# An adaLN block with Hedgehog attention and a ReLU feed-forward: moving the feature work of two blocks ahead wholly into FFN1, and its attention products to the second and eighth part of FFN2

## The chip, the cores and the metric

The kernel runs on one core of a Trainium2 chip. The metric is the device time of one execution in microseconds (us), taken as the median over runs. Beside it stands one profiled execution, from which all durations of single instructions come.

## The reference, cut to what matters

```python
# S = 2048 rows, D = 576, H = 32 heads of 18, Dff = 4608, bf16 inputs
mod = (silu(c) @ w_mod).reshape(1, 6, 1, 576);  sa, ca, ga, sb, cb, gb = its six rows
h = layernorm(x) * (1 + ca) + sa
q, k, v = split(h @ wqkv)                                  # per head
phi(t) = concat(softmax(t @ w_phi), softmax(-(t @ w_phi)))  # 36 features a head
kv = phi(k)^T v;  z = sum over rows of phi(k)
o = (phi(q) kv) / (phi(q) z + 1e-6)
x = x + ga * (o @ wo)
h = layernorm(x) * (1 + cb) + sb
out = x + gb * (relu(h @ w1) @ w2)
```

## The kernel before

The 2048 rows are 16 tiles of 128. A first part (some 130 us) folds the modulation into the weights, projects all queries, keys and values, and builds `kv`. After it the rows go through in eight **blocks** of two tiles (`n` = 0 to 7, 256 rows each). Block 0 is part of a hand-written list of steps; blocks 1 to 7 are calls of `block(n)`. The program writes the order of TensorE (PE), VectorE (DVE), ScalarE (ACT) and of the DMA queue on SyncE (SP) by hand: each engine takes its instructions strictly as the code issues them, and waits only on semaphores.

A block has two stages on PE. **FFN1** (`ffn1_rows`) makes nine tiles `ps_h` of hidden units, each in an a-half and a b-half of the weight rows; they are issued as a0, a1, b0, a2, b1, ... a8, b7, b8. After each b-half ACT empties the tile with a ReLU (`f1_relu`, L872) into `H1`. The pool behind `ps_h`, `ps_y` has three buffers. A dictionary `behind` names what is issued right behind a given half: `("b", 5)` means behind the b-half of tile 5 and its ReLU. **FFN2** is twelve **parts** of twelve matmuls (`ffn2_step(n, j, cs, cn, part)`, L910): for each of the two row tiles `j` and each half of the columns `cs`, three parts; behind the third, DVE multiplies by the gate and adds the residual (L918, L919).

Between these matmuls three blocks are worked on at once. While block `n` is on PE:

- for block `m = n + 1`: the attention output projection (`wo_rows`, in two halves of rows, tile `ps_wo`), the residual `wo_out` and the row statistics `stats` (together `late`), and then `norm_out`: `rstd` on ACT (a logarithm and an exponential, L233, L234), `norm` and a copy on DVE (L238, L423) and two DMA transposes on SP into `hT` (L425). `mods` (L418 on DVE) then applies shift and scale to `hT`, which FFN1 of the next block reads.
- for block `n + 2`: the **features** of its queries in a buffer that the profile calls `room`: `low` and `high` (DVE), `exps(0)` and `exps(1)` (ACT, L506), `sums(0)` and `sums(1)` (DVE, L524, into `ln_s`), `recip` (ACT, L529 and L531, into `rsum`), `scale` (DVE, L541), `q_T` (two DMA transposes on SP into `ET`, one for each row tile, L653). Then `attention(n + 2, j)`: the products `num` on PE (L666: eleven small matmuls that read `ET`, into `ps_num` and `ps_nun`), `quotient` on DVE (L674 to L681) and a DMA transpose `o_T` on SP (L689).

Blocks 1 to 5 have all of this; block 6 has no features to make (`n + 2` is past the end), block 7 neither. In block 1 the attention of block 2 also falls into FFN1.

Of the kernel before, what the change touches and what calls it, by code (L numbers as in the profile page):

```python
# [21 lines left out]
NQ = NT // U  # L22
# [21 lines left out]
def kernel(  # L44
# [34 lines left out]
    def mm_tile(name):  # L79
        return mmp.tile([P, 2, 512], FP32, name=name, tag="mm")  # L80

    def aux_tile(name, dt=FP32):
        t = aux.tile([P, 512], FP32, name=name, tag="aux")
        return t if dt == FP32 else t.bitcast(BF16)
# [365 lines left out]
    HALVES = [(0, 288), (288, 288)]  # L450
# [148 lines left out]
    def q_soft(n):  # L599
        E = Eqs[n % 2]  # L600
        if n < 2:
            G.memset(E[:, :, :, DW:], 0.0)
        Es[n] = E
        b, u = n // 2, n % 2
        return softmax_parts(E[:, :, :, 0:DW], pq[b][:, u * U:(u + 1) * U], U, False)
# [42 lines left out]
    def q_T(n):  # L648
        E = Es[n]
        ET = work.tile([P, NG, U, P], BF16, name="ET", tag="ET", bufs=2)  # L650
        ETs[n] = ET
        for j in range(U):
            nc.sync.dma_start_transpose(out=ET[:, :, j, :], in_=E[:, j].rearrange("p g c -> p (g c)"))  # L653

    def num(n, j):

        ET = ETs[n]
        if n == 0:
            ps = mm_tile("ps_num")
            ps = (ps[:, 0], ps[:, 1])  # L660
        else:
            ps = (aux_tile("ps_num"), aux_tile("ps_nun"))
        onum[n, j] = ps
        for g in range(NG):
            o = (g % GB) * GV
            T_.matmul(ps[g // GB][:, o:o + gcols(g)], lhsT=ET[0:DW, g, j, :], rhs=KVZ[0:DW, g, 0:gcols(g)],  # L666
                      start=True, stop=True)
# [156 lines left out]
    def row_halves(key, phase, items):  # L824

        for k, (ps, l, r) in enumerate(items):
            i = T_.matmul(ps, lhsT=l, rhs=r, start=(phase == 0 and k < 2), stop=(phase == 1 and k >= len(items) - 2))  # L827
            if phase == 1 and k == 0:
                tc.add_manual_dep(i.ins, last[key].ins.name, AFTER, reason="same banks, other rows")
        if phase == 0:  # L830
            g = last[key] = G.memset(token[:], 0.0)  # L831
            tc.add_manual_dep(g.ins, i.ins.name, AFTER, reason="products of one half of the rows done")

    def f1_rows(n, q, phase):

        hT, w, items = hT2[n], U * P, []
        if phase == 0:
            f1_open(n, (q,))
        for hh in range(2):
            for ci in ((4, 0, 1, 2, 3) if phase == 0 else (0, 1, 2, 3)):  # L840
                for r in range(2):
                    s, e = slice(r * 64, r * 64 + 64), r ^ phase
                    l = w1["c"][s, 2 * q + hh, :] if ci == 4 else w1_at(2 * q + hh, e, ci, s)
                    items.append((f1[q][:, e, hh * w:hh * w + w], l, hT[s, ci, :]))
        row_halves(("f1", q), phase, items)

    def wo_rows(n, j, phase):

        if phase == 0:
            onum["wo", n, j] = [aux_tile("ps_wo") for _ in HALVES]  # L850
        items = []
        for ci in ((4, 0, 1, 2, 3) if phase == 0 else (0, 1, 2, 3)):
            for r in range(2):
                s, e = slice(r * 64, r * 64 + 64), r ^ phase
                items.append((onum["wo", n, j][e][:, 0:288], oTs[n, j][s, ci, :], wo_sb[s, ci, e * 288:e * 288 + 288]))
        row_halves(("wo", j), phase, items)

    def ffn1_rows(n, behind={}):

        for k in range(NI // 2 + 1):  # L860
            for p in (0, 1):
                q = k - p
                if k == 0 and p == 1 or q > NI // 2 - 1:
                    continue
                f1_rows(n, q, p)
                if p:
                    f1_relu(q)
                if ("ab"[p], q) in behind:
                    behind["ab"[p], q]()

    def f1_relu(q):
        A_.activation(out=p2t["H1"].rearrange("p (e j) n -> p e j n", e=2)[:, :, 2 * q:2 * q + 2],  # L872
                      in_=f1[q][:].rearrange("p e (h n) -> p e h n", h=2), func=ACT.Relu)
# [27 lines left out]
    def ffn2_step(n, j, cs, cn, part):  # L901

        if part == 0:
            f2[j, cs] = mm_tile("ps_y")
            if ("o", n, j) not in f2:
                f2["o", n, j], f2["sent"] = p2t["p2"].tile([P, D], BF16, name="outt", tag="outt", bufs=2), 0
        ps, o = f2[j, cs], f2["o", n, j]
        c = slice(cs, cs + cn)
        for k in [e * NI + part * 6 + i for e in range(2) for i in range(6)]:
            T_.matmul(ps[:, 0, 0:cn], lhsT=p2t["H1"][:, k, j * P:(j + 1) * P], rhs=p2t["w2"][:, k, c],  # L910
                      start=(k == 0), stop=(k == NJ - 1))
        if part == 2 and n > 0:
            ffn2_out(n, j, cs, cn)

    def ffn2_out(n, j, cs, cn):
        ps, o = f2[j, cs], f2["o", n, j]
        c = slice(cs, cs + cn)
        V.tensor_tensor(out=o[:, c], in0=ps[:, 0, 0:cn], in1=rows["gb"][:, c], op=ALU.mult)  # L918
        V.tensor_tensor(out=o[:, c], in0=o[:, c], in1=x_sb[:, n * U + j, c], op=ALU.add)  # L919
        if cs + cn == D or (n, j) == (NQ - 1, U - 1):  # L920
            nc.sync.dma_start(outv[:, n * U + j, f2["sent"]:cs + cn], o[:, f2["sent"]:cs + cn])
            f2["sent"] = cs + cn if cs + cn < D else 0

    def y(n, j, cols=HALVES):
        for cs, cn in cols:
            for part in range(3):
                ffn2_step(n, j, cs, cn, part)
# [74 lines left out]
    def block(n):  # L1002


        m = n + 1 if n + 1 < NQ else None
        if m is None:
            ffn1_rows(n)
            y(n, 0)

            y(n, 1, ((0, 288), (288, 192), (480, 96)))  # L1010
            return
        soft_ = q_soft(n + 2) if n + 2 < NQ else None
        xn, stats, rstd, norm = norm_stats(m * U, U)

        def do(name, *a):
            if soft_ is not None:
                getattr(soft_, name)(*a)

        def attention(m, j):
            num(m, j)  # L1020
            quotient(m, j)
            o_T(m, j)

        def late(j):
            wo_rows(m, j, 1)
            wo_out(m, j)
            stats(j)

        def norm_out():
            rstd()  # L1030
            norm()
            norm_dma(xn, U, new_hT2(m), 0)

        def mods():
            for ci in range(KC):
                modulate(V, hT2[m][:, ci, :], hT2[m][:, ci, :], mod[2], ci)

        def both(*fs):
            return lambda: [f() for f in fs]

        if n == 1:
            do("low")
            do("high")
            ffn1_rows(n, {("b", 0): lambda: attention(m, 0), ("b", 2): lambda: attention(m, 1), ("b", 3): lambda: do("exps", 0),
                          ("b", 4): both(lambda: wo_rows(m, 0, 0), lambda: do("exps", 1)), ("b", 5): both(lambda: late(0), lambda: do("sums", 0)),
                          ("a", 8): lambda: wo_rows(m, 1, 0), ("b", 7): lambda: late(1)})
        else:
            ffn1_rows(n, {("a", 0): both(lambda: do("low"), lambda: do("high")), ("b", 1): lambda: wo_rows(m, 0, 0),
                          ("b", 2): lambda: late(0), ("b", 3): lambda: do("exps", 0), ("b", 4): both(lambda: wo_rows(m, 1, 0), lambda: do("exps", 1)),
                          ("b", 5): both(lambda: late(1), lambda: do("sums", 0))})  # L1050
        norm_out()
        do("sums", 1)
        y(n, 0, HALVES[:1])
        do("recip", 0)
        do("scale", 0)
        if n + 2 < NQ:
            q_T(n + 2)
        ffn2_step(n, 0, 288, 288, 0)
        mods()
        ffn2_step(n, 0, 288, 288, 1)  # L1060
        ffn2_step(n, 0, 288, 288, 2)
        ffn2_step(n, 1, 0, 288, 0)
        if n + 2 < NQ:
            attention(n + 2, 0)
        ffn2_step(n, 1, 0, 288, 1)
        ffn2_step(n, 1, 0, 288, 2)
        ffn2_step(n, 1, 288, 288, 0)
        if n + 2 < NQ:
            attention(n + 2, 1)
        ffn2_step(n, 1, 288, 288, 1)  # L1070
        ffn2_step(n, 1, 288, 288, 2)

    for n in range(1, NQ):
        block(n)
# [28 lines left out]
```

## Time and profile before

| | |
|---|---|
| time, median of 3 runs | 415.11 us (414.38 to 416.61) |
| profiled execution: its own time | 414.88 us |
| profiled execution: its span | 413.1 us (1.8 us lie around it) |
| DVE, ACT busy share of the span | 57%, 43% |
| FFN1 of blocks 1 to 7 begins at | 140.6, 181.9, 220.8, 259.4, 298.1, 336.7, 374.4 us |

Times within the profile are microseconds from the start of the span. A timeline row has start, duration, engine, line, instruction, tiles (output <- inputs), shape and the number of instructions merged; what stands in brackets at its end is the idle time of that engine before it and what ended it. A row of the chain of waits has start, duration, engine, tile and line: it is the sequence of work that ended last.

### The profile page before, as it was taken

To read this page: it belongs to the slowest core of one execution; us is meant where nothing else is said; L and a number is where in the kernel's file an instruction comes from. 1 tells how busy PE (TensorE), PEld (TensorE's weight loads), DVE (VectorE), ACT (ScalarE), POOL (GpSimd) and SP (SyncE) were. 2 spreads that over 40 slices of the span, in tenths; PEclk is the share of its full clock that TensorE was granted. 3 is DMA by queue.
4 is the path that set the end of the run, shared out by engine and by line. 5 is a ranking of instruction groups with operands and counts; after the bars stand their busy time and mean duration, and the time that the engine had idled before them with its cause. 6 is when DMAs were issued, how large, how long until landed. Compare 5 with 4: busy or idle time off the path is not lost.

```text
span 413.1 us, 11585 instructions
## 1 busy us (share of the span) xinstructions
PE 402.8 (98%) x5064; PEld 329.8 (80%) x5064; DVE 234.5 (57%) x600; ACT 178.6 (43%) x303; POOL 17.8 (4%) x112
## 2 busy tenths in 40 slices
PE   6999999999999999899999999999999999999997
PEld 3777777787887888688878887887788788878876
DVE  6889999989838556563566355536553731230011
ACT  5799999945751064006401530262046004402500
POOL 7100000000000000000000000000000000000000
PEclk9999999999999999999999999999999999999999
DMA  8967950499670630720061014105400520010000
GB/s 263 268 111 206 197 126 17 88 279 369 222 173 18 130 37 2 117 48 2 17 116 35 3 33 100 33 2 65 86 17 4 116 48 3 17 30 17 2 2 29
DMA packets 70988, 35.58 MB, mean 86 GB/s; under 512 B 56657, under 2 KB 67418, under 8 KB 70938
## 3 DMA queue, kind: packets, MB, share of 16 engines
q1 hardware_dynamic: 70336, 34.83, 36.2%
q8 instruction: 39, 0.64, 0.7%
q10 hardware_dynamic: 602, 0.02, 0.1%
q14 instruction: 11, 0.09, 0.1%
HBM read 19.27 MB, written 2.37 MB: 52 GB/s over the span
## 4 chain that ended last, share of the span: by engine, by line
PE 87%; DMA 8%; DVE 3%; issue 0%; SPq 0%; ACT 0%
PE ps_h L827 30%; PE ps_y L910 27%; DMA ET<-room 5%; PE ps_v L447 5%; PE ps_k L447 5%; PE ps_q L447 4%; PE ps_h L818 4%; PE ps_wo L827 3%; PE ps_sum L513 2%; DMA wma<-in_w_mod_dram 2%; DVE room L541 2%; PE ps_kv L625 1%; DMA kv_raw<-in_A_wqkv_dram 1%; PE ps_wo L447 1%; PE ps_num L666 1%; DVE outt L918 1%
## 5 line engine op out<-in xcount | busy, mean ns | idle before, releaser
L872 ACT ACTIVATE H<-ps_h 128x1024 bf16<-128x1024 f32 x72 | 72.7, 1022 | 172.2 <-PE ps_h L827 168.7
L910 PE MATMUL ps_y<-w_sb,H 128*128 128x288 bf16 (+2 forms) x1188 | 144.7, 282 | 0.0
L910 PEld LDWEIGHTS <-H 128*128 128x128 bf16 x1188 | 112.3, 98 | 28.1 <-issue 1.5
L827 PE MATMUL ps_h<-hT,w1a 64*128 64x256 bf16 x1120 | 70.9, 269 | 0.0
L827 PEld LDWEIGHTS <-w1a 64*128 64x128 bf16 x1120 | 54.5, 94 | 6.7
L827 PE MATMUL ps_h<-hT,w1b 64*128 64x256 bf16 x896 | 56.4, 269 | 0.0
L447 PEld LDWEIGHTS <-hT 128*128 128x128 bf16 x480 | 45.9, 97 | 12.6 <-issue 0.5
L918 DVE TENSOR_TENSOR outt<-ps_y,row_gb 128x288 bf16<-128x288 f32 (+2 forms) x33 | 14.8, 448 | 62.0 <-PE ps_y L910 61.9
L827 PEld LDWEIGHTS <-w1b 64*128 64x128 bf16 x896 | 43.6, 94 | 5.5
L728 DVE TENSOR_TENSOR x_sb<-x_sb,ps_wo 128x288 bf16<-128x288 bf16 x28 | 11.6, 451 | 53.3 <-PE ps_wo L827 52.0
L827 PE MATMUL ps_h<-hT,w1c 64*128 64x256 bf16 x252 | 34.4, 270 | 0.0
L238 DVE TENSOR_SCALAR xn<-x_sb,mv,rstd 128x576 bf16<-128x576 bf16 x32 | 12.3, 426 | 19.5 <-ACT rstd L234 19.4
L447 PE MATMUL ps_v<-wv_sb,hT 128*128 128x288 bf16 x160 | 21.6, 286 | 0.0
L447 PE MATMUL ps_q<-wfold,hT 128*128 128x270 bf16 (+1 forms) x160 | 21.4, 285 | 0.0
L447 PE MATMUL ps_k<-wfold,hT 128*128 128x270 bf16 (+1 forms) x160 | 21.4, 285 | 0.0
L831 POOL MEMSET token<- 1x2 bf16 x75 | 6.7, 89 | 336.4 <-PE ps_h L827 320.6
L506 ACT ACTIVATE room<-room 128x1188 bf16<-128x1188 bf16 x16 | 19.0, 1191 | 1.5 <-DVE room L479 1.5
L226 DVE BATCH_NORM_STATS2 bst<-x_sb 128x6 f32<-128x288 bf16 x46 | 18.5, 445 | 1.1 <-DMA x_sb<-in_A_x_dram 1.1
L524 DVE TENSOR_REDUCE ln_s<-room 128x66 f32<-128x1188 bf16 x14 | 19.0, 1366 | 0.0
L506 ACT ACTIVATE phik<-phik 128x2376 bf16<-128x2376 bf16 x8 | 17.4, 2186 | 0.0
L827 PE MATMUL ps_wo<-wo_sb,oT 64*128 64x288 bf16 x216 | 17.2, 283 | 0.0
L466 DVE TENSOR_TENSOR tree<-tree 128x264 bf16<-128x264 bf16 (+2 forms) x48 | 14.6, 305 | 1.7
(154 smaller groups left out, 400.5 us busy)
## 6 DMA issues: line engine op xcount, KB each, us to landing
w_sb<-in_B_w_dram SPq DMA_DIRECT2D x6, 864.0 KB, 7.5
out_dram<-outt SPq DMA_DIRECT2D x15, 144.0 KB, 1.8
w1b<-in_B_w_dram SPq DMA_DIRECT2D x2, 1024.0 KB, 9.6
x_sb<-in_A_x_dram SPq DMA_DIRECT2D x3, 576.0 KB, 7.3
w1a<-in_B_w_dram SPq DMA_DIRECT2D x2, 768.0 KB, 4.7
kv_raw<-in_A_wqkv_dram SPq DMA_DIRECT2D x4, 288.0 KB, 5.0
wma<-in_w_mod_dram SPq DMA_DIRECT2D x1, 1152.0 KB
wmb<-in_w_mod_dram SPq DMA_DIRECT2D x2, 576.0 KB, 4.1
```

The lines of the kernel that those rows point to most:

```text
L226: V.bn_stats(out=st[:, half, :], in_=x_sb[:, t0 + j, half * 288:(half + 1) * 288])
L238: V.tensor_scalar(out=xn[:, j, 0:D], in0=x_sb[:, t0 + j, :], scalar1=mv[:, j, 0:1], scalar2=rs[:, j:j + 1], op0=ALU.subtract if by[j] == " ...
L447: T_.matmul(ps[:, 0:cn], lhsT=lhs[:, ci, :], rhs=w[:, ci, cs:cs + cn], start=(ci == 0), stop=(ci == KC - 1))
L466: V.tensor_tensor(out=a[:, :, 0:w], in0=a[:, :, 0:w], in1=a[:, :, w:2 * w], op=op)
L506: A_.activation(out=E[:, j:j + k], in_=E[:, j:j + k], func=ACT.Exp)
L524: V.tensor_reduce(out=t["l", b][:, k * 22:(k + 1) * 22].rearrange("p (g s) h -> p g s h", s=2), op=ALU.add, axis=mybir.AxisListType.X, in_ ...
L728: V.tensor_tensor(out=xs[:, cs:cs + cn], in0=xs[:, cs:cs + cn], in1=p[:, 0:cn], op=ALU.add)
L818: T_.matmul(f1[q][:, e, hh * w:hh * w + w], lhsT=w1_at(2 * q + hh, e, ci), rhs=hT[:, ci, :], start=(first and hh == 0 and ci == 0), stop=( ...
L827: i = T_.matmul(ps, lhsT=l, rhs=r, start=(phase == 0 and k < 2), stop=(phase == 1 and k >= len(items) - 2))
L872: A_.activation(out=p2t["H1"].rearrange("p (e j) n -> p e j n", e=2)[:, :, 2 * q:2 * q + 2], in_=f1[q][:].rearrange("p e (h n) -> p e h n" ...
L910: T_.matmul(ps[:, 0, 0:cn], lhsT=p2t["H1"][:, k, j * P:(j + 1) * P], rhs=p2t["w2"][:, k, c], start=(k == 0), stop=(k == NJ - 1))
L918: V.tensor_tensor(out=o[:, c], in0=ps[:, 0, 0:cn], in1=rows["gb"][:, c], op=ALU.mult)
```

## The change

The orders of blocks 1 to 6 are written anew. In FFN1, `exps` are issued one place earlier, both `sums`, `recip`, `scale` and the transposes `q_T` (now `turn`) are all issued within FFN1, and for blocks 2 to 6 `norm_out` too, behind the b-half of tile 5. In FFN2 the products of block `n + 2` are issued ahead of the parts (0, 0, 1) and (1, 0, 1), so behind the first and the seventh part (before: behind the seventh and the tenth), and `mods` ahead of part (0, 288, 1).

```diff
         if n == 1:
             do("low")
             do("high")
-            ffn1_rows(n, {("b", 0): lambda: attention(m, 0), ("b", 2): lambda: attention(m, 1), ("b", 3): lambda: do("exps", 0),
-                          ("b", 4): both(lambda: wo_rows(m, 0, 0), lambda: do("exps", 1)), ("b", 5): both(lambda: late(0), lambda: do("sums", 0)),
-                          ("a", 8): lambda: wo_rows(m, 1, 0), ("b", 7): lambda: late(1)})
+            ffn1_rows(n, {("b", 0): lambda: attention(m, 0), ("b", 2): both(lambda: attention(m, 1), lambda: do("exps", 0)),
+                          ("b", 3): lambda: do("exps", 1), ("b", 4): both(lambda: wo_rows(m, 0, 0), lambda: do("sums", 0)),
+                          ("b", 5): both(lambda: late(0), lambda: do("sums", 1), lambda: do("recip", 0)), ("a", 8): lambda: wo_rows(m, 1, 0),
+                          ("b", 7): both(lambda: do("scale", 0), lambda: late(1), turn)})
+            norm_out()
         else:
             ffn1_rows(n, {("a", 0): both(lambda: do("low"), lambda: do("high")), ("b", 1): lambda: wo_rows(m, 0, 0),
-                          ("b", 2): lambda: late(0), ("b", 3): lambda: do("exps", 0), ("b", 4): both(lambda: wo_rows(m, 1, 0), lambda: do("exps", 1)),
-                          ("b", 5): both(lambda: late(1), lambda: do("sums", 0))})
-        norm_out()
-        do("sums", 1)
-        y(n, 0, HALVES[:1])
-        do("recip", 0)
-        do("scale", 0)
-        if n + 2 < NQ:
-            q_T(n + 2)
-        ffn2_step(n, 0, 288, 288, 0)
-        mods()
-        ffn2_step(n, 0, 288, 288, 1)
-        ffn2_step(n, 0, 288, 288, 2)
-        ffn2_step(n, 1, 0, 288, 0)
-        if n + 2 < NQ:
-            attention(n + 2, 0)
-        ffn2_step(n, 1, 0, 288, 1)
-        ffn2_step(n, 1, 0, 288, 2)
-        ffn2_step(n, 1, 288, 288, 0)
-        if n + 2 < NQ:
-            attention(n + 2, 1)
-        ffn2_step(n, 1, 288, 288, 1)
-        ffn2_step(n, 1, 288, 288, 2)
+                          ("b", 2): both(lambda: late(0), lambda: do("exps", 0)), ("b", 3): lambda: do("exps", 1),
+                          ("b", 4): both(lambda: wo_rows(m, 1, 0), lambda: do("sums", 0)),
+                          ("b", 5): both(lambda: late(1), lambda: do("sums", 1), norm_out), ("b", 6): lambda: do("recip", 0),
+                          ("b", 7): both(lambda: do("scale", 0), turn)})
+        for j, cs, part in ((0, 0, 0), (0, 0, 1), (0, 0, 2), (0, 288, 0), (0, 288, 1), (0, 288, 2),
+                            (1, 0, 0), (1, 0, 1), (1, 0, 2), (1, 288, 0), (1, 288, 1), (1, 288, 2)):
+            if (j, cs, part) == (0, 288, 1):
+                mods()
+            if part == 1 and cs == 0 and n + 2 < NQ:
+                attention(n + 2, j)
+            ffn2_step(n, j, cs, 288, part)
```

`turn` calls `q_T(n + 2)` where that block exists.

On DVE, at the passage from FFN1 to FFN2 in block 4 (`mv` are the row statistics, `ln_s` the sums of `sums(1)` or `sums(0)`, `xn` the normed rows, `rq` the first step of `quotient`). Before:

```order
L227 BN_AGGR mv_4372<-bst_4699 128x2
L524 TENSOR_REDUCE ln_s_4703<-room_100 128x66
L238 TENSOR_SCALAR xn_4374<-x_sb_79,mv_4372,rstd_4373 128x576 x2
L423 COPY xn_4374<-xn_4374 128x2x64
L524 TENSOR_REDUCE ln_s_4703<-room_100 128x66
L918 TENSOR_TENSOR outt_4810<-ps_y_4809,row_gb_1939 128x288
L919 TENSOR_TENSOR outt_4810<-outt_4810,x_sb_79 128x288
L541 TENSOR_TENSOR room_100<-room_100,rsum_4850 128x22x54 x2
L418 TENSOR_SCALAR hT2_4804<-hT2_4804,mod2_171 128x256 x5
L918 TENSOR_TENSOR outt_4810<-ps_y_4857,row_gb_1939 128x288
L919 TENSOR_TENSOR outt_4810<-outt_4810,x_sb_79 128x288
L674 TENSOR_SCALAR rq_4929<-ps_num_4916 128x24
```

And now, on the same engine at the same place:

```order
L227 BN_AGGR mv_4372<-bst_4701 128x2
L524 TENSOR_REDUCE ln_s_4650<-room_100 128x66
L238 TENSOR_SCALAR xn_4374<-x_sb_79,mv_4372,rstd_4373 128x576 x2
L423 COPY xn_4374<-xn_4374 128x2x64
L541 TENSOR_TENSOR room_100<-room_100,rsum_4754 128x22x54 x2
L674 TENSOR_SCALAR rq_4844<-ps_num_4831 128x24
L674 TENSOR_SCALAR rq_4844<-ps_nun_4832 128x8
L675 RECIPROCAL rq_4844<-rq_4844 128x32
L678 TENSOR_TENSOR o_tm_4848<-ps_num_4831,rq_4844 128x432
L678 TENSOR_TENSOR o_tm_4848<-ps_nun_4832,rq_4844 128x144
L681 COPY o_tm_4848<-o_tm_4848 128x64
L918 TENSOR_TENSOR outt_4818<-ps_y_4817,row_gb_1939 128x288
```

The scaling L541 stands right behind the norm, and the quotient of the first products ahead of the first output of FFN2; before, one output lay ahead of the scaling, and a second one and `mods` between it and the quotient.

On ACT, in FFN1 of the same block (each L872 is the ReLU of one `ps_h` tile; the first row is that of tile 3 before and the exponential behind tile 2 now). Before:

```order
L872 ACTIVATE H1_1822<-ps_h_4504 128x2x512
L506 ACTIVATE room_100<-room_100 128x11x108
L872 ACTIVATE H1_1822<-ps_h_4557 128x2x512
L506 ACTIVATE room_100<-room_100 128x11x108
L872 ACTIVATE H1_1822<-ps_h_4597 128x2x512
L872 ACTIVATE H1_1822<-ps_h_4650 128x2x512
L872 ACTIVATE H1_1822<-ps_h_4705 128x2x512
L872 ACTIVATE H1_1822<-ps_h_4744 128x2x512
L233 ACTIVATE rstd_4373<-mv_4372,eps_t_113 128x2
L234 ACTIVATE rstd_4373<-rstd_4373 128x2
L529 ACTIVATE ln_s_4703<-ln_s_4703 128x132
L531 ACTIVATE rsum_4850<-ln_s_4703 128x264
```

And now:

```order
L506 ACTIVATE room_100<-room_100 128x11x108
L872 ACTIVATE H1_1822<-ps_h_4504 128x2x512
L506 ACTIVATE room_100<-room_100 128x11x108
L872 ACTIVATE H1_1822<-ps_h_4558 128x2x512
L872 ACTIVATE H1_1822<-ps_h_4598 128x2x512
L233 ACTIVATE rstd_4373<-mv_4372,eps_t_113 128x2
L234 ACTIVATE rstd_4373<-rstd_4373 128x2
L872 ACTIVATE H1_1822<-ps_h_4652 128x2x512
L529 ACTIVATE ln_s_4650<-ln_s_4650 128x132
L531 ACTIVATE rsum_4754<-ln_s_4650 128x264
L872 ACTIVATE H1_1822<-ps_h_4714 128x2x512
L872 ACTIVATE H1_1822<-ps_h_4756 128x2x512
```

The pair L233, L234 now stands ahead of the ReLU of tile 6, and the pair L529, L531 behind it; before, both stood behind the last ReLU.

More of the change, by code (lines that the diff above doesn't have):

```diff
@@ L1039, in both, with turn @@
             return lambda: [f() for f in fs]
+        def turn():
+            if n + 2 < NQ:
+                q_T(n + 2)
         if n == 1:
```

## The prediction

> **What bounds the kernel now.** I read the page first, then PE's waits, then the timelines of PE, DVE, ACT and SP in one middle block (block 4), and the chain of waits there. The page, part 1 and the clock row of part 2, and the longest entry of PE's waits:
>
> ```profile
> PE 402.8 (98%) x5064; PEld 329.8 (80%) x5064; DVE 234.5 (57%) x600; ACT 178.6 (43%) x303; POOL 17.8 (4%) x112
> PEclk9999999999999999999999999999999999999999
> PE ps_num L666 <- DMA ET<-room: 2.1, 2, 1.7
> ```
>
> PE is busy 98% of the span. What it still loses in the blocks are waits for `ET` ahead of the attention products. PE's timeline shows where; rows of blocks 1, 2 and 4:
>
> ```profile
> 161.60 10.46 PE L910 MATMUL ps_y<-w_sb,H 128*128 128x288 bf16 x84
> 173.79 0.40 PE L666 MATMUL ps_num<-KVZ,ET 108*128 108x57 bf16 x8 [1.73 <-DMA ET<-room]
> 174.12 4.57 PE L910 MATMUL ps_y<-w_sb,H 128*128 128x288 bf16 x36
> 201.87 4.34 PE L910 MATMUL ps_y<-w_sb,H 128*128 128x288 bf16 x34
> 212.75 0.41 PE L666 MATMUL ps_num<-KVZ,ET 108*128 108x57 bf16 x8 [0.41 <-DMA ET<-room]
> 274.05 0.65 PE L827 MATMUL ps_wo<-wo_sb,oT 64*128 64x288 bf16 x8
> 279.44 10.46 PE L910 MATMUL ps_y<-w_sb,H 128*128 128x288 bf16 x84
> ```
>
> and the chain of waits through block 4:
>
> ```profile
> 286.30 3.63 DMA ET<-room
> 289.97 0.40 PE ps_num L666 x8
> 290.45 4.42 PE ps_y L910 x36
> ```
>
> 36 FFN2 matmuls take 4.42 us, so one takes 0.123 and a part of twelve 1.47 us. Seven parts are 10.31 us: in block 4 the products are due at 279.44 + 10.31 = 289.75 and begin at 289.97, so even there 0.22 us are lost. The same sum gives 1.88 us in block 1 (161.60 to 173.79) and 0.57 in block 2 (201.87 to 212.75). Taking 0.22 for blocks 3 and 5 as well, **all that this wait costs is 3.1 us**. That is the most the change can win: PE's matmuls stay the same in number and kind.
>
> **The change part by part.** The price is decided by one question: when does `ET` land, against products that are now due behind one part, 1.47 us into FFN2. I lay the new order over block 4. Its rows on DVE, then ACT, then SP (the first two of SP are from the end of block 0):
>
> ```profile
> 276.32 0.21 DVE L227 BATCH_NORM_AGGREGATE mv<-bst 128x2 f32<-128x12 f32 x1
> 276.45 1.34 DVE L524 TENSOR_REDUCE ln_s<-room 128x66 f32<-128x1188 bf16 x1
> 281.06 0.77 DVE L238 TENSOR_SCALAR xn<-x_sb,mv,rstd 128x576 bf16<-128x576 bf16 x2 [3.27 <-ACT rstd L234]
> 281.87 0.20 DVE L423 COPY xn<-xn 128x128 bf16<-128x128 bf16 x1
> 284.77 1.46 DVE L541 TENSOR_TENSOR room<-room,rsum 128x1188 bf16<-128x1188 bf16 x2
> ```
>
> ```profile
> 274.25 1.02 ACT L872 ACTIVATE H<-ps_h 128x1024 bf16<-128x1024 f32 x1 [0.44 <-PE ps_h L827]
> 276.71 1.02 ACT L872 ACTIVATE H<-ps_h 128x1024 bf16<-128x1024 f32 x1 [1.43 <-PE ps_h L827]
> 278.67 1.94 ACT L872 ACTIVATE H<-ps_h 128x1024 bf16<-128x1024 f32 x2 [0.94 <-PE ps_h L827]
> 280.50 0.30 ACT L233 ACTIVATE rstd<-mv,eps_t 128x2 f32<-128x2 f32 x1
> 280.82 0.20 ACT L234 ACTIVATE rstd<-rstd 128x2 f32<-128x2 f32 x1
> 283.39 0.31 ACT L529 ACTIVATE ln_s<-ln_s 128x132 f32<-128x132 f32 x1 [2.36 <-DVE ln_s L524]
> 283.74 0.42 ACT L531 ACTIVATE rsum<-ln_s 128x264 bf16<-128x264 f32 x1
> ```
>
> ```profile
> 134.07 2.76 SPq L425 DMA_TRANSPOSE hT<-xn  x2
> 136.92 3.12 SPq L653 DMA_TRANSPOSE ET<-room  x2
> 282.12 2.97 SPq L425 DMA_TRANSPOSE hT<-xn  x2
> 286.30 3.11 SPq L653 DMA_TRANSPOSE ET<-room  x2
> ```
>
> The first thing that cannot move is `late(1)`: it needs the second half of `ps_wo`, issued on PE at 274.05, and its statistics end at 276.53. Then:
>
> - DVE: `sums(1)` 276.45 + 1.34 = 277.79 (its exponentials are older than before, so they are there).
> - ACT: ReLU 5 ends at 275.27; L233, L234 wait for the statistics, 276.56 to 277.08; ReLU 6, which began at 276.71, now 277.05 to 278.05; `recip` (283.39 to 284.16, 0.77 us) from 278.0 to 278.77. ReLU 7 slips from 278.67 to about 278.75.
> - DVE: norm and copy, 1.01 us from 277.79, end at 278.77; `scale` 278.8 to 280.3.
> - SP: the `hT` transposes go at 278.8 and hold the queue 2.5 to 3.0 us, to 281.35 or later. Only then comes the first `ET` transpose, at 281.4, though its data were ready at 280.3. It lands 3.63 us later, at **285.05**.
>
> FFN2 starts at 279.44, so the products are due at 280.91. **PE stalls 4.14 us.** PE takes matmuls in order, as block 1 shows: the `ps_y` matmuls behind the products waited with them, to 174.12. So the whole stall goes to the end, and in blocks 2 to 5 alike: 4 x 4.14 = 16.6 us. The stall repeats from block to block because everything in the chain hangs on this block's own `ps_wo`.
>
> Block 1 is ordered otherwise (`scale` ahead of `late(1)`, `ET` ahead of `hT`). Its rows on DVE, on ACT, and the `ET` transposes of blocks 1 and 2 on SP:
>
> ```profile
> 157.51 1.34 DVE L524 TENSOR_REDUCE ln_s<-room 128x66 f32<-128x1188 bf16 x1
> ```
>
> ```profile
> 155.31 1.02 ACT L872 ACTIVATE H<-ps_h 128x1024 bf16<-128x1024 f32 x1 [0.44 <-PE ps_h L827]
> ```
>
> ```profile
> 168.46 3.14 SPq L653 DMA_TRANSPOSE ET<-room  x2
> ...
> 208.73 3.98 SPq L653 DMA_TRANSPOSE ET<-room  x2
> ```
>
> `sums(1)` takes that place and ends at 158.85; `recip` sits ahead of ReLU 6 and runs to 159.65, `scale` to 161.15, the first `ET` lands at 161.2 + 3.63 = 164.8; due at 161.60 + 1.47 = 163.07: a stall of 1.8 us.
>
> **Queue hiccups.** Four of the six passages (blocks 0 to 5) took longer than the best, 2.5 us for `hT` on the queue and 3.6 for `ET` to land: block 1's `ET` needed 173.79 - 168.46 = 5.3 us, block 2's 212.75 - 208.73 = 4.0, block 4's `hT` held the queue 2.97, block 0's 2.76. That is 2.8 us over six, 0.45 each, and the new chain runs through both kinds of transposes: 5 x 0.45 = 2.2 us. The bounds are 0 and 1.7 us a block.
>
> Edits at nothing: the earlier exponentials fill gaps of ACT; `mods` stays eight parts, 11.8 us, ahead of the FFN1 that needs it; the second products come six parts behind the first, with `ET` landed; block 6 only has its norm earlier. A ReLU that is late does no harm as long as its tile is free in time: ReLU 6 must be over when FFN2 takes its buffer at 279.44, and ends at 278.05 (1.4 us of cover; in block 1 0.9).
>
> **Sum** on the profiled execution: 414.88 - 3.1 + 16.6 + 1.8 + 2.2 = 432.4. The median of the runs lies 0.2 above that execution: **432.6 us**, 4% more.
>
> **A rule against it, and the rivals.** While PE stood still for 1.73 us in block 1, it lost no speed (36 matmuls in 4.57 us right behind). But its first microseconds show a slower PE, with the clock row at 9 all along:
>
> ```profile
> 6.76 2.16 PE L335 MATMUL ps_wT<-ident,kv_raw 128*108 128x128 bf16 x18 [1.69 <-DMA kv_raw<-in_A_wqkv_dram]
> ...
> 9.78 0.63 PE L203 MATMUL ps_warm<-zeros 128*128 128x512 bf16 x1
> ...
> 11.97 0.38 PE L203 MATMUL ps_warm<-zeros 128*128 128x512 bf16 x1
> ...
> 13.40 0.72 PE L262 MATMUL psT_h<-ident,xn 128*128 128x128 bf16 x10
> ```
>
> 128-wide products took about 0.11 us each at 6.76 and 0.05 at 13.40; a 512-wide one 0.63 and later 0.38. So PE after idling runs at half its rate until 3.0 to 5.2 us of work are done.
>
> *Rival 1, PE cools in the stalls.* A stall of over 4 us is longer than any in this trace, so it may end in that slow state. Price 1.5 to 2.6 us a stall (half of 3.0 to 5.2), 6 to 10 in all four: 438 to 442; one to three of four: 434 to 438. Against it: nothing here shows what length of stall suffices. The Trainium skill ("TensorE: Matmul & The Clock Gate", Part 1) says that PE falls to half clock after at least one idle window of about 3.4 us, that the windows run free of the kernel, and that one busy window restores it. By that rule a stall of 4.1 us holds a whole window only sometimes; were it each time, the sum would be an estimated 432.6 + 4 x 1.7 = 439. The trace agrees as far as its start goes; no row here shows a warm PE falling back. Chance 0.23.
>
> *Rival 2, `ET` lands in time.* Then only the 3.1 us go: 412.0, faster. It decides at 285.05 against 280.91: `ET` would have to be issued by 277.3, while `recip` cannot end before 277.79 + 0.77. Even with `hT` behind it on SP, 1.1 us of the 4.1 would go, no more. Chance 0.03.
>
> *Rival 3, a wait inside FFN1.* ACT now stands for DVE in the middle of the ReLUs (L233 waits for the statistics; in block 1 L529 for the sums, 158.85). If it holds ReLU 6 over 1.4 us longer than worked out (0.9 in block 1), PE waits for a `ps_h` buffer on top; up to 1 us in five blocks, 433 to 437. The rows leave cover, so 0.08.
>
> That the products run under later matmuls, and the stall vanishes to about 415, contradicts the in-order rows of block 1: 0.02.
>
> **How the numbers follow.** My forecast has 0.64, the rivals 0.23, 0.03, 0.08 and 0.02. The forecast's own range: landings of 3.5 us and no hiccups give 4 x 4.0 + 1.6 - 3.1, 429.5; less 1 us for a queue that is quicker than its rows, 428.5; with 1 us a block of hiccups 435.5. Half of rival 1 must be in for 8 in 10: 440 at the top. A measurement of this kernel can tell 0.5% (2 us) from no change; faster by more has rival 2, 0.03; same 0.02; slower 0.95.
>
> **What would show it.** Right: PE's waits list `ps_num <- DMA ET<-room` with five entries of about 2 (once) and 4 to 4.6 us, blocks 2 to 5 take 42.7 to 43.2 us instead of 38.6, the first `ET` issues right behind `hT` on SP, ReLUs never end a wait of PE. Wrong: no such waits, or `ps_h` and `ps_y` waiting for ACT; FFN2 matmuls behind the stall at 0.25 us each would be rival 1.

## The result, and the profile after

The changed kernel takes **437.87 us** (median of 6 runs, 437.06 to 440.24) against 415.47 for the kernel before in the same set: a ratio of **1.055**, 95% interval 1.0518 to 1.0583. The profiled execution takes 440.24 us with a span of 438.4; it is the slowest of the six. In several kernels here, the one before included, part of the runs have a mean clock of 0.995 or 0.996 and not 1.000, and those of the kernel before take about 2 us more.

The page after, part 1, the clock row, and the first entry of PE's waits (total, times, longest):

```profile
PE 412.8 (94%) x5063; PEld 333.8 (76%) x5064; DVE 234.3 (53%) x600; ACT 178.3 (41%) x303; POOL 18.7 (4%) x112
PEclk9899999999999999999699969998999899999999
PE ps_num L666 <- DMA ET<-room: 17.6, 5, 4.0
```

Before, this wait had two entries and 2.1 us. Now it has one for each of the blocks 1 to 5. The clock row, all 9 before, dips once near the start and four times from 208 us on, and PE's busy time is 10 us longer for the same matmuls. So there are two losses: PE stands still, and PE is slow.

PE's timeline shows both (blocks 1, 2 and 4):

```profile
163.14 1.64 PE L910 MATMUL ps_y<-w_sb,H 128*128 128x288 bf16 x12
166.42 0.41 PE L666 MATMUL ps_num<-KVZ,ET 108*128 108x57 bf16 x8 [1.63 <-DMA ET<-room]
166.75 8.98 PE L910 MATMUL ps_y<-w_sb,H 128*128 128x288 bf16 x72
203.32 1.64 PE L910 MATMUL ps_y<-w_sb,H 128*128 128x288 bf16 x12
208.97 0.57 PE L666 MATMUL ps_num<-KVZ,ET 108*128 108x57 bf16 x8 [4.00 <-DMA ET<-room]
209.50 11.61 PE L910 MATMUL ps_y<-w_sb,H 128*128 128x288 bf16 x72
293.58 1.65 PE L910 MATMUL ps_y<-w_sb,H 128*128 128x288 bf16 x12
299.21 0.41 PE L666 MATMUL ps_num<-KVZ,ET 108*128 108x57 bf16 x8 [3.98 <-DMA ET<-room]
```

In block 4 the products are due at 293.58 + 1.47 = 295.05 and start at 299.21: 4.16 us. In block 1 the same sum gives 1.8. Behind block 1's stall 72 FFN2 matmuls take 8.98 us, behind block 2's 11.61.

Why `ET` is late, in block 4: rows on DVE, ACT and SP.

```profile
290.47 0.21 DVE L227 BATCH_NORM_AGGREGATE mv<-bst 128x2 f32<-128x12 f32 x1
290.60 1.33 DVE L524 TENSOR_REDUCE ln_s<-room 128x66 f32<-128x1188 bf16 x1
291.85 0.76 DVE L238 TENSOR_SCALAR xn<-x_sb,mv,rstd 128x576 bf16<-128x576 bf16 x2
292.64 0.20 DVE L423 COPY xn<-xn 128x128 bf16<-128x128 bf16 x1
292.84 1.47 DVE L541 TENSOR_TENSOR room<-room,rsum 128x1188 bf16<-128x1188 bf16 x2
```

```profile
290.71 0.29 ACT L233 ACTIVATE rstd<-mv,eps_t 128x2 f32<-128x2 f32 x1 [1.29 <-DVE mv L227]
291.04 0.20 ACT L234 ACTIVATE rstd<-rstd 128x2 f32<-128x2 f32 x1
291.15 1.00 ACT L872 ACTIVATE H<-ps_h 128x1024 bf16<-128x1024 f32 x1
292.39 0.42 ACT L531 ACTIVATE rsum<-ln_s 128x264 bf16<-128x264 f32 x1
```

```profile
292.90 2.52 SPq L425 DMA_TRANSPOSE hT<-xn  x2
295.53 3.14 SPq L653 DMA_TRANSPOSE ET<-room  x2
```

The statistics, `sums(1)`, norm and scaling stand back to back on DVE; the scaling ends at 294.31. SP is then still busy with `hT`, and `ET` is issued at 295.53, 1.2 us after its data are ready and 0.5 us after its products are due. The chain of waits has this piece in blocks 2 to 5 (here 2 and 4):

```profile
203.41 0.44 SPq L425
203.91 1.27 SPq L425
205.28 3.64 DMA ET<-room
208.97 0.57 PE ps_num L666 x8
209.53 0.13 PE ps_nun L666 x3
209.66 11.45 PE ps_y L910 x72
...
295.53 3.63 DMA ET<-room
299.21 0.41 PE ps_num L666 x8
299.69 10.50 PE ps_y L910 x72
```

The slow stretch is the clock, not a wait. Stretches of 0.7 us through block 2 (after the length: busy time of PE, the matmuls that touch the stretch, granted clock, mean busy share of the DMA engines, GB/s):

```profile
207.20:207.90 0.70, 0.00 (x0) 1.00 1.12 208
207.90:208.60 0.70, 0.00 (x0) 0.62 1.07 197
...
214.20:214.90 0.70, 0.70 (x5) 0.51 0.00 0
214.90:215.60 0.70, 0.70 (x8) 1.00 0.00 0
```

The clock halves while PE is still idle, and comes back at about 214.9: 5 matmuls touch the stretch before, 8 the one behind.

**Where the 25.4 us between the two profiled executions went** (440.24 - 414.88). Stalls: 1.8 + 4.2 + 3 x 4.15 = 18.4. Half clock: the chain has 72 matmuls at 11.45, 10.96, 10.50 and 10.49 us in blocks 2 to 5, against 8.84 at full clock (two times 4.42 for 36): 8.0. The waits of before are gone: -3.1. Ahead of all this FFN2 of block 1 starts 1.5 us later (163.14 for 161.60), because in this execution PE also ran at half clock from about 17 to 20 us, in work that the change does not touch. Together 24.8; some 0.3 more is the products themselves at half clock, and 0.3 stay open.

The granted clock tells what the other five runs had. One slow stretch lasts 3.41 us (last section), which at half clock takes 0.0039 off the mean of a span of 438 us. The profiled run's 0.973 is seven of them: one near the start, two each in blocks 2 and 3, one each in blocks 4 and 5. The six runs lie between 0.973 and 0.984, so they had four to seven. Where they lay in the five that were not profiled is not shown.

### The profile page after: what moved, and what is told of

Its sections match the earlier page's. It is cut to its first block, busy times and chain, and to the rows that moved or that the text cites. A ratio compares the mean times of both kernels' runs of the same rounds, so it can differ in the third digit from the quotient of the medians.

```text
span 438.4 us, 11591 instructions
## 1 busy us (share of the span) xinstructions
PE 412.8 (94%) x5063; PEld 333.8 (76%) x5064; DVE 234.3 (53%) x600; ACT 178.3 (41%) x303; POOL 18.7 (4%) x112
## 4 chain that ended last, share of the span: by engine, by line
PE 88%; DMA 7%; SPq 2%; DVE 1%; ACT 1%; issue 0%
PE ps_y L910 32%; PE ps_h L827 27%; PE ps_v L447 5%; PE ps_k L447 5%; PE ps_q L447 4%; DMA ET<-room 4%; PE ps_h L818 4%; PE ps_wo L827 3%; PE ps_sum L513 2%; DMA wma<-in_w_mod_dram 2%; SPq L425 2%; PE ps_num L666 1%; PE ps_kv L625 1%; PE ps_wo L447 1%; DMA kv_raw<-in_A_wqkv_dram 1%; PE ps_bias L366 1%
## 5 line engine op out<-in xcount | busy, mean ns | idle before, releaser
L872 ACT ACTIVATE H<-ps_h 128x1024 bf16<-128x1024 f32 x72 | 72.5, 1021 | 199.2 <-PE ps_h L827 195.7
L910 PE MATMUL ps_y<-w_sb,H 128*128 128x288 bf16 (+2 forms) x1188 | 152.8, 292 | 0.0
L910 PEld LDWEIGHTS <-H 128*128 128x128 bf16 x1188 | 115.9, 101 | 32.7 <-issue 1.5
L666 PE MATMUL ps_num<-KVZ,ET 108*128 108x57 bf16 (+1 forms) x134 | 7.2, 196 | 17.7 <-DMA ET<-room 17.6
L666 PEld LDWEIGHTS <-ET 108*128 108x128 bf16 x176 | 7.1, 101 | 20.2 <-DMA ET<-room 19.1
L674 DVE TENSOR_SCALAR rq<-ps_num 128x24 f32<-128x24 f32 (+1 forms) x18 | 3.1, 179 | 34.4 <-PE ps_num L666 34.3
```

## The experiments

The theory: all that the change loses is the stall of the first products on a late `ET`, and the half clock behind it. Rivals: FFN1's new order costs by itself; or the slow matmuls are not from idleness.

**FFN1's half of the change alone** (`ffn1_only`): the new FFN1, with the products where they were.

```diff
-            if part == 1 and cs == 0 and n + 2 < NQ:
-                attention(n + 2, j)
+            if (j, cs, part) in ((1, 0, 1), (1, 288, 1)) and n + 2 < NQ:
+                attention(n + 2, cs // 288)
```

> The new order of FFN1 alone: the products go back behind the seventh and the tenth part of FFN2, all else is as in the changed kernel. Theory (the whole loss is the wait of the first products for ET, and PE's half clock behind that wait): ET lands about 5.6 us into FFN2, the products are due at 10.3, so no wait is left in blocks 1 to 5 and no half clock; the 3.1 us that the kernel before lost go as well: about 412, ratio 0.992. Rival (ACT and DVE crowded in FFN1, or SP's transposes in FFN1, cost time of their own): 416 or more, with PE waiting for ACT in FFN1.

Measured: **411.15 us** (6 runs, 410.77 to 411.70), ratio 0.9895 with 0.9868 to 0.9922. This beats both kernels. PE's timeline in block 4, and then the first entry of PE's waits:

```profile
276.29 10.46 PE L910 MATMUL ps_y<-w_sb,H 128*128 128x288 bf16 x84
286.59 0.40 PE L666 MATMUL ps_num<-KVZ,ET 108*128 108x57 bf16 x8
```

```profile
PE ps_warm L203 <- DVE ccol L166: 1.2, 1, 1.2
```

The products come exactly when due (276.29 + 10.31), and no wait for `ET` is left; the longest wait is now one of the first microseconds. The profiled execution is 414.88 - 411.21 = 3.7 us shorter; 0.4 of it lies ahead of block 1's FFN2 (161.16 for 161.60), so the blocks gained 3.2. FFN1's new order costs nothing: that rival is out. The ratio shows a little more than 3.2 us: all runs of this kernel had a mean clock of 1.000, while half of those of the kernel before lay at 0.995 to 0.996 and 1.5 to 2 us higher.

**FFN2's half alone** (`attention_only`): FFN1 as before, then the rest of the feature work in one go. The edit is against the kernel before.

```diff
         norm_out()
         do("sums", 1)
-        y(n, 0, HALVES[:1])
         do("recip", 0)
         do("scale", 0)
...
+        turn()
+        for j, cs, part in ((0, 0, 0), (0, 0, 1), ...     # FFN2 as in the changed kernel
```

> The new order of FFN2 alone: FFN1 as in the kernel before, then norm, second sums, recip, scaling and the ET transposes in one go, then FFN2 with its products at the second and eighth part. Theory (a stall is ET's landing less the moment the products are due): by the rows before, ET lands 8.5 us behind that moment in blocks 1 to 5, 42 us in all; each stall is followed by a half clock worth about 2 us, 10 in all: 412 + 52 = 464, between 458 and 470. So the FFN1 half of the change is worth some 26 us against the FFN2 half. Rival (the products' place decides, and FFN1's order does not matter): 438, as the changed kernel.

Measured: 462.82 us (one run). PE's waits, and block 2 on PE's timeline:

```profile
PE ps_num L666 <- DMA ET<-room: 41.5, 5, 8.3
```

```profile
219.70 0.57 PE L666 MATMUL ps_num<-KVZ,ET 108*128 108x57 bf16 x8 [8.31 <-DMA ET<-room]
220.23 10.07 PE L910 MATMUL ps_y<-w_sb,H 128*128 128x288 bf16 x72
```

Five stalls of 8.3, each with a slow stretch behind, near the 464 that the theory gave; the rival's 438 is out. The new FFN1 is worth some 25 us against this (one run), and still leaves `ET` late. With the new FFN1 the loss hangs on the place of the products.

**One place further on** (`behind_3`, `behind_2`): the first products behind the third or the second part.

```diff
-            if part == 1 and cs == 0 and n + 2 < NQ:
+            if (j, cs, part) in ((0, 288, 0), (1, 0, 1)) and n + 2 < NQ:   # behind_2: (0, 0, 2) for (0, 288, 0)
```

> The changed kernel with the first products behind the third part of FFN2 instead of the first (the second ones stay behind the seventh). Theory: two parts are 2.95 us, so the stall in blocks 2 to 5 falls from 4.15 to 1.2 us and the one of block 1 goes; a stall this short leaves PE at full clock (1.63 and 1.73 us did): 412 + 4 x 1.2 = 416.8, ratio 1.003, granted clock as in the kernel before. Rival (products early in FFN2 cost by themselves, whatever ET does): over 420.

Measured: 418.72 us (10 runs), ratio 1.0069 with 1.0045 to 1.0093; the profiled one 417.21. PE's timeline, blocks 2 and 5:

```profile
205.22 0.41 PE L666 MATMUL ps_num<-KVZ,ET 108*128 108x57 bf16 x8 [1.06 <-DMA ET<-room]
205.55 6.04 PE L910 MATMUL ps_y<-w_sb,H 128*128 128x288 bf16 x48
325.07 0.41 PE L666 MATMUL ps_num<-KVZ,ET 108*128 108x57 bf16 x8 [2.09 <-DMA ET<-room]
```

The stall is 1.06 us in blocks 2 to 4; in block 5 a transpose came 1 us late. The 48 matmuls behind it take 6.04 us, full clock. The profiled execution agrees with the 416.8 expected, and the rival's 420 is not reached: early products cost nothing but their wait. The median lies 1.5 above it: four of the ten runs, with a mean clock of 1.000, took 416.7 to 417.3, the other six, at 0.992 to 0.996, up to 420.6; where the clock fell in those is not shown.

> The changed kernel with the first products behind the second part of FFN2. Theory: one part less, so the stall in blocks 2 to 5 is 2.68 us, block 1's 0.3: 411.5 + 10.7 + 0.3 = 422.5 at full clock. Clock: in the traces so far PE fell to half clock wherever 2.16 us or more of a stall lay within one stretch of a 3.4 us grid, and not at 1.95 or less. By that a stall of 2.68 us brings the half clock in something over half of the cases, each worth 1.6 us: 424 to 428, and the clock changes at the grid's marks. Rival (a whole stretch of 3.4 us must be idle): no half clock in blocks 2 to 5, 422.5.

Measured: 428.60 us (4 runs), ratio 1.0309 with 1.026 to 1.0359: 0.6 above what the theory gave, 6 above the rival. Stretches of 3 us around the stalls of blocks 2 and 3, of 2.54 and 2.52 us (after the length: PE, its weight loads, DVE, ACT and POOL, then the granted clock and the DMA engines; the second row of each pair is behind the products):

```profile
204.00:207.00 3.00, 0.67 (x6) 0.29 (x3) 0.00 (x0) 0.00 (x0) 0.00 (x0) 1.00 0.89 169
208.00:211.00 3.00, 3.00 (x14) 1.92 (x13) 1.84 (x6) 0.00 (x0) 0.00 (x0) 0.50 0.20 40
247.00:250.00 3.00, 0.47 (x6) 0.15 (x4) 0.00 (x0) 0.00 (x0) 0.00 (x0) 1.00 0.91 173
250.50:253.50 3.00, 3.00 (x27) 2.38 (x26) 2.86 (x11) 0.00 (x0) 0.00 (x0) 1.00 0.22 45
```

Stalls of one length, and once 14 matmuls touch the 3 us behind, once 27. Two of the four stalls brought the half clock, those of blocks 2 and 5, and the one in block 5 was 3.43 us long, again a transpose that came late. From the 422.5 at full clock: two times 1.67 for 60 matmuls in 9.18 us and not 7.51, 0.9 for the late transpose, and 1.6 because FFN2 of block 1 begins at 162.83 and not at 161.20 as in `behind_3` (here too the clock is halved early, from 16.6 to 20.0 us). That makes 428.3; the profiled execution took 428.33.

**PE kept at work in the stall** (`keep_warm`): matmuls without use, into the tile that the products overwrite.

```diff
+        if j == 0 and n > 3:
+            for _ in range(18):
+                T_.matmul(ps[0][:], lhsT=ident[:], rhs=wo_sb[:, 0, 0:512], start=True, stop=True)
         for g in range(NG):
```

> The changed kernel with 18 matmuls of 512 columns ahead of the first products in blocks 2 to 5, into the tile that the products overwrite; about 3.9 us of work that fills the stall of 4.15 us and ends before ET lands. It adds work that is not in the reference's computation and changes no result. Theory: the stall stays, the half clock behind it goes: 437.9 less about 7.5, so 430 to 431, ratio 1.036, and the 72 FFN2 matmuls behind the products take 8.84 us instead of 10.5 to 11.5. Rival (the slow stretch comes from the ET and oT transposes or from PSUM, not from idleness): 437 to 438, slow stretch as before.

Measured: 432.28 us (4 runs, 430.28 to 432.54), ratio 1.0392 with 1.0357 to 1.0428: 5.6 us less than the changed kernel with 72 matmuls more. PE's timeline, block 2 (L666 is here the added line, the products are L669):

```profile
204.64 4.05 PE L666 MATMUL ps_num<-wo_sb,ident 128*128 128x512 bf16 x17
208.81 0.41 PE L669 MATMUL ps_num<-KVZ,ET 108*128 108x57 bf16 x8
209.14 8.98 PE L913 MATMUL ps_y<-w_sb,H 128*128 128x288 bf16 x72
```

The 72 matmuls are back at 8.98 us in all four blocks. In blocks 2, 3 and 5 `ET` is issued 1.95 us behind the start of FFN2, as in the changed kernel, and the first `oT` at most 0.2 us sooner; so it is idleness, not traffic, that slows PE. In block 4 a transpose came 1 us late, and PE idled 1.15 us behind the added matmuls without losing its clock. The median is 1 to 2 us above the expectation: three of the four runs have a mean clock of 0.995 or 0.996 (in the profiled one it is halved from 16 to 20 us, and nowhere else); the one at 1.000 took 430.28.

**SP's order** (`et_first`): `ET` ahead of `hT` on SP, in blocks 2 to 6.

```diff
-            norm_dma(xn, U, new_hT2(m), 0)
+            V.tensor_copy(out=xn[:, 0:U, D:], in_=xn[:, 0:U, 512:D])   # the transposes of norm_dma: norm_turn
...
-                          ("b", 7): both(lambda: do("scale", 0), turn)})
+                          ("b", 7): both(lambda: do("scale", 0), turn, norm_turn)})
```

> The changed kernel with the transposes of ET ahead of those of hT on SP in blocks 2 to 6. Theory: ET is issued when the scaling ends, 1.05 us sooner, and the stall in blocks 2 to 5 falls from 4.15 to 3.1 us: 4.2 us less. What the clock then does is open: if a stall needs about 2 us within one stretch of the clock's 3.4 us grid, most of the four still bring the half clock (430 to 434); if it needs 3.4 us of idleness, none does: about 426. Rival (SP's order does not matter, ET is late for its scaling): 437 to 438.

Measured: 429.09 us (4 runs), ratio 1.0329 with 1.0297 to 1.0362, 8.8 us less than the changed kernel. PE's timeline, blocks 2 and 3:

```profile
206.31 0.52 PE L666 MATMUL ps_num<-KVZ,ET 108*128 108x57 bf16 x8 [2.82 <-DMA ET<-room]
206.80 10.45 PE L910 MATMUL ps_y<-w_sb,H 128*128 128x288 bf16 x72
249.31 0.41 PE L666 MATMUL ps_num<-KVZ,ET 108*128 108x57 bf16 x8 [2.83 <-DMA ET<-room]
249.64 8.98 PE L910 MATMUL ps_y<-w_sb,H 128*128 128x288 bf16 x72
```

The stall falls by 1.15 us a block, 4.6 in all, so the rival is out: SP's order matters. The rest is half clock. Between the profiled executions (440.24 and 428.81) it came behind two stalls (blocks 2 and 4) and not four, for 3.1 us and not 8.1, and the early half clock, 1.5 us, is absent in this one. Neither of the two cases written down for the clock came out whole; the truth lay between.

## Why the prediction was right, and where it was not

- *The most the change can win, 3.1 us*: held. The FFN1 half alone won 3.2.
- *The stall, 4.14 us in blocks 2 to 5 and 1.8 in block 1*: held, 4.15 to 4.2 and 1.8. The chain came out as laid over block 4: after `late(1)` it is DVE, ACT and SP back to back, and SP's `hT` transposes decide the last 1.1 us.
- *No new wait in FFN1* (rival 3 did not come): held. ReLU 6 was over at 292.15, 1.4 us ahead of FFN2, as worked out; PE's waits name no ACT in the blocks.
- *Queue hiccups, 0.45 us a block*: the term was too large. The profiled execution had none (`hT` 2.52 us on the queue, `ET` landing in 3.63). Over the twenty passages in blocks 2 to 5 of the five kernels with early products (all but `attention_only`), three came about 1 us late: 0.15 each. In `ffn1_only`, where PE does not wait for them, two of four pairs of `ET` transposes held the queue 0.9 to 1.2 us longer than the others. What makes them late stays open.
- *The choice between the forecast and rival 1*: this is the step that failed. The forecast took a full clock behind the stalls as likeliest, at 0.64 against 0.23; the half clock came behind all four, for 8.0 us. Its price was right (1.5 to 2.6 us a stall; measured 1.65 to 2.6). The sign that went with the forecast, 42.7 to 43.2 us a block, failed with it: from FFN2 to FFN2, blocks 2 and 3 took 45.4 and 44.9.
- *The sum*: that 437.87 lies in the range is in part luck, for two errors offset each other. Against the 432.4 for the profiled execution the runs showed 8.3 more for half clock (the products included), 1.5 more for the early stretch that the change does not touch, and 2.2 less, for hiccups that did not come: 440.0 for 440.24. The 438 to 442 written for rival 1 hold those 2.2 us as well, and the median lies just below them. The range held it because it took in half of that rival. Without the half clock and without the hiccups the sum is 430.2; the run of `keep_warm` with a mean clock of 1.000 took 430.28.
- What misled was to hold that a stall of 4.1 us meets the condition only sometimes, since a whole clock window would have to be idle. The runs show that less suffices (below).

## What to carry to other kernels

Moving a consumer forward pays only up to the moment its operand lands: add up the whole chain, the other transfers on the same queue included, from the last event that cannot move, and place the consumer behind that. Here feeding the chain earlier won 3.2 us (0.8%), and calling the consumer earlier on top of it turned that into 5% lost. A long stall of PE has to be priced twice, once as idle time and once as slow work behind it. In the profiled executions here no stall for `ET` of up to 2.1 us brought the half clock, three of seven of 2.5 to 2.8 us did, and all ten of 3.4 us and more.

## What the runs showed of the hardware that was not expected

In the changed kernel the clock falls or rises near 208.1, 214.9, 252.4, 259.3, 300.2, 303.6, 344.6 and 348.0 us: the differences are multiples of 3.41 (44.4 is 13 steps, 47.8 is 14). So in this trace the clock changes only at the marks of a fixed grid. Two of the marks in slices of 0.1 us, and the 3.4 us ahead of the early half clock (PE alone, columns as above):

```profile
252.40:252.50 0.10, 0.00 (x0) 0.70 1.11 225
300.20:300.30 0.10, 0.10 (x3) 0.63 0.52 103
13.50:16.90 3.40, 2.68 (x67) 1.00 1.12 261
```

The Trainium skill ("TensorE: Matmul & The Clock Gate", Part 1) says that the clock is set by windows of about 3.4 us that run free of the kernel, and that PE falls to half clock after at least one idle window. The trace agrees with the length of the window and with the half rate, not with a whole idle window: PE fell behind stalls of 2.5 and 2.8 us.

Laying each run's grid over its stalls, the idle time in one stretch was 2.1 us or more wherever PE fell (the four stalls of the changed kernel, two of `et_first`, two of `behind_2`), and 1.95 us or less wherever it did not (the other two of each). The least, in block 3 of the changed kernel, is 252.44 - 250.34 = 2.10; the 2.16 in the expectation of `behind_2` is a little high. A stall of over 4.2 us lies on two stretches or more and so always leaves 2.1 us in one; by this bound it always costs. That some 2 us of 3.4 suffice fits these twelve stalls, and the other stalls for `ET` do not speak against it; the bound was not measured by itself.

Idle time is not all that counts, though. The early half clock, from 16.9 us on, came with no such stall: in the 3.4 us ahead of it PE was busy for 2.68 us, but 50 of its 67 matmuls there have a single column (`ps_mod`, L313). What counts there was not tested, so the bound holds for stalls between FFN2 matmuls.

The slow stretch ends at the first mark behind a stretch that is full, or nearly: one stretch late in blocks 4 and 5 (10.5 us for 72 matmuls), two in blocks 2 and 3, where the products began after the mark. In `attention_only` 0.64 us of idle time at the start of a stretch still let the clock rise at its end (block 2); 0.90 us in block 2 of the changed kernel did not.
